# Linear attention and squared-ReLU MLP in one kernel: the written-out order of all five engines replaced by another

## Chip, cores and metric

One core of a Trainium2 chip runs the whole program. The metric is the device time of one execution in microseconds (us), as a median over executions. Engine names are those of the profile: PE is TensorE, PEld its weight loads, DVE is VectorE, ACT is ScalarE, POOL is GpSimd, SP is SyncE, which here issues the DMAs.

## What is computed

```python
def phi(x):                                  # x: 8 batches, 8 heads, 576 tokens, 64 wide
    proj = einsum('bhsd,df->bhsf', x, w_phi) # 128 features
    proj = proj - max(abs(proj), axis=-1, keepdims=True)
    return concatenate([exp(proj), exp(-proj)], axis=-1)
q_p, k_p = phi(q), phi(k)
kv = einsum('bhsf,bhsd->bhfd', k_p, v)
z = sum(k_p, axis=2)
num = einsum('bhsf,bhfd->bhsd', q_p, kv)
den = einsum('bhsf,bhf->bhs', q_p, z)[..., None] + 1e-06
x = (num / den) as 4608 tokens x 512
g = maximum(x @ w_in, 0) ** 2                # w_in 512 x 2048
out = g @ w_out                              # w_out 2048 x 512
```

## The kernel before

The work is cut into items. `P.add` records an item with its engine, a duration that the planner assumes, the items it must follow, the buffers and PSUM banks it uses, and a class of TensorE use (WHOLE, ROWS, COLS, STRIPS: the whole array, or parts of its rows or columns). There are 3676 items, 590 of them on PE. Nothing is scheduled at run time: the string ORDER holds two characters for each item, its place in one list over all engines, and the string WAYS holds one digit for each item that can run on more than one engine. `Plan.order` sorts the items by place; each engine then executes its own in that sequence, and the Tile layer puts semaphore waits where the data or a buffer demand one. So an engine that waits holds up everything behind it on that engine. DMAs all go out from SP, in the same fixed sequence.

Attention goes by 32 pairs of heads. Pairs 0 to 5 (`early`, lines 607 to 742) are done while the weights are still being prepared. For each: `k_main` and `k_tail` (L532, L538) and `q_main` and `q_tail` (L655, L661) multiply keys and queries by w_phi; DVE takes the row maxima and subtracts them (L548, L551, L559, L562 for keys, L666, L668 for queries); ACT makes the exponentials of the keys (L554, L556, L565, L567); `kv_main` and `ends` (L594, L599, L627) make kv and z; `flip` (L639) and `q_turn` (L689, L693) transpose; ACT makes the exponentials of the queries out of PSUM (L698, L700); `num` and `dens` (L708, L725) make numerators and denominators. The next product into the PSUM pair `pp` must wait until L698 and L700 have read it. Pairs 6 to 31 (`visit`, `late`) do the same with larger items between the MLP's.

Also in the first 100 us the 16 blocks of the MLP's weights (1 MB each, tiles raw0i to raw7i and raw0o to raw7o) are loaded and brought into split form: ACT and POOL each process the raw words (L399, L402), DVE joins them (L406), POOL and DVE write the parts (L442, L249, L460, L471, L474). `power` (L341 on PE, then four small DVE instructions L347, L348, L351, L352) finds a power of two to scale two weight blocks by.

The MLP runs over 18 chunks of 256 tokens. The first four go by `gemm1` (L956, 24 matmuls) and `gemm2` (L993, 12 matmuls); the other 14 go in pairs by a block scheme with seven products instead of eight (`step`, L1161) and `gemm2`. Intermediate halves are put away to memory and read back by SP.

In `tile_kernel`'s last lines, where the plan leaves a gap of over 0.7 us on PE in the first 125 us and a PSUM bank is free, matmuls on a zero tile (`zeros`, L1332) are put into it; the first eight such matmuls (`warm`, L359) stand at the very start.

```python
        order = sorted(self.ops, key=lambda op: place[op.n])
...
            if last and last.end < FILL_TO and op.start - last.end > 0.7:
                gaps.append((last.end, op.start))
...
        fills.append((t0, lambda tag=free[0], n=n, count=int(0.6 * (t1 - t0) / 0.214): zeros(tag, n, count)))
```

Of the kernel before, what the change touches and what calls it, by code (L numbers as in the profile page):

```python
# [235 lines left out]
def tile_kernel(ctx, tc, qp, kp, vp, w_phi, w_in, w_out, out):  # L236
    nc = tc.nc
    V, A, G, PE, SP = nc.vector, nc.scalar, nc.gpsimd, nc.tensor, nc.sync
    P = Plan()
# [365 lines left out]
    def early(p):  # L605
# [26 lines left out]
        o = P.add("PE", 1.7, lambda: kv_main(p, pv_["s", p]), exps[p] + [v_load[p]], kv[:-1], R(2.0), mode=COLS)  # L632
        o = P.add("PE", 1.76, ends, [o, exp_t[p]], kv, R(2.5), mode=(COLS, STRIPS))
# [48 lines left out]
        for c in range(2):  # L682
# [13 lines left out]
            o = P.add("PE", 0.7, q_turn, [pool_start] + less[:2 + c], [pq, ("pt", p)], R(x), mode=(WHOLE, ROWS if c else WHOLE))  # L696
# [104 lines left out]
    def visit(i):  # L801
# [60 lines left out]
        if n is not None:  # L862
            v3 = visited[0] = P.add("PE", 2.04, numerators, [kz_of[n]] + qexp[n], use_n, R(0.0), mode=COLS)
# [80 lines left out]
    def moe(c, f, turn, n, m, po):  # L944
# [15 lines left out]
        g1 = P.add("PE", 2.61, gemm1, after, [("ph", bank), (f"w{f}", 0)], m)  # L960
# [20 lines left out]
    def second(n, c, v, f, turn, g, rank, po):  # L981
# [189 lines left out]
    def step(cs, k, turn, f, n, m):  # L1171
# [193 lines left out]
    "#k#s#z#}$&#?#F#n#V#x$9$D$M$$$:$<$]$e$i%(%.%6%>%2%;%=%R%V%j%}&*&8!b#Q#(#W#8#=#E#|#N#`#r$+#^#m$4$5$2$;"
    "$L$c$o$,$?$f$b$j$u%#%%$m$y%)%-%8%B%h&$%m&&%M%T%X%d%g%r&-&3&6#q#a$B$F$6$C$v&4&h&}($(B*}#J$K#f$*#{$)$I"
    "$Q$#$1$@$k$.$0$N$z$w$}%0%C%N$p%&%4%7%:%<%H%K%b%l%n%q%x&!&9&>&5&n&(&,&/&:&Y&l(%(|)#(x)0#c%D$E$Z$O$R%5"
    "%E$U$X$r%1$[$^$n$t%Q%Z%e&+&0&1&?&A&F&L&B&U&Z&O&S&W&^&e&g(-(3(K(R(G(L(Z(i(m(z)D)L)Q)S)x$J%I%G%@%P%U%_"
    "%i%Y%^%s%v%L%a%c%p%u&)&%%F(4(8&k%y(>(F(H&y&|(0&z(((.(;()(,(9(D&X&p&_&s)&);),&M(`(?(o(v(})$)()))5)F)]"
# [107 lines left out]
```

## Time and profile before

| what | us |
|---|---|
| median of 3 executions | 1010.53 |
| lowest and highest | 1009.52, 1014.01 |
| the profiled execution | 1009.59 |
| its span, first to last instruction | 1007.8 |
| PE busy (with modelled ends) | 993.1 |
| DVE, ACT, POOL busy | 801.9, 605.3, 352.5 |

Busy times are unions of an engine's instructions. Matmuls are pipelined and their ends are modelled, so a matmul that was held up for less than its own pipeline's length shows no idle time; starts are exact, and from the start of one item to the start of the next is the time that the item took on PE.

### The profile page before, as it was taken

The numbers are of one execution on the slowest core, as the hardware profiler recorded it, in microseconds if no ns is written. First come the engines' busy times: TensorE is split into PE (matmuls) and PEld (weight loads), VectorE is DVE, ScalarE is ACT, GpSimd is POOL, SyncE is SP. The second block draws the span as 40 slices with busy tenths as digits, with TensorE's granted clock in tenths as the row PEclk, the third lists the DMA queues.
The fourth block names the chain that finished last, engine by engine and source line by source line (L and its number), as shares of the span: only waits on it lengthen the run. The fifth ranks groups of instructions, "written<-read, shape, count | busy, mean of one in ns | idle before, by whom it ended". The sixth has DMA issues, their size and how long they took to land.

```text
span 1007.8 us, 19886 instructions
## 1 busy us (share of the span) xinstructions
PE 993.1 (99%) x7552; PEld 676.4 (67%) x7552; DVE 801.9 (80%) x1417; ACT 605.3 (60%) x1140; POOL 352.5 (35%) x141
## 2 busy tenths in 40 slices
PE   9899999999999999999999999999999999999998
PEld 5666666666677776676657775677567756766774
DVE  6899888899997788887898988778878775773543
ACT  6798876766654576477765775476825552441232
POOL 2562366556510154443373543533452420000000
PEclk9999999999999999999999999999999999999999
DMA  9865532542235776667676685568756655666321
GB/s 340 300 193 181 170 95 81 156 146 71 60 114 164 215 230 197 211 196 218 211 200 202 192 272 173 175 184 245 207 149 185 193 180 191 223 203 216 105 84 42
DMA packets 149543, 180.60 MB, mean 179 GB/s; under 512 B 76872, under 2 KB 97352, under 8 KB 147400
## 3 DMA queue, kind: packets, MB, share of 16 engines
q1 hardware_dynamic: 149160, 178.81, 57.6%
q8 instruction: 59, 0.97, 0.4%
q10 hardware_dynamic: 288, 0.52, 0.1%
q14 instruction: 36, 0.29, 0.1%
HBM read 137.93 MB, written 41.21 MB: 178 GB/s over the span
## 4 chain that ended last, share of the span: by engine, by line
PE 82%; DVE 7%; issue 4%; DMA 2%; ACT 2%; POOL 1%; SPq 0%; POOLq 0%; DVEq 0%; ACTq 0%
PE po L993 32%; PE ph L1161 9%; PE ph L956 7%; PE pv L1161 6%; PE pn L1161 6%; PE pz L594 4%; PE pn L830 2%; PE pp L532 2%; PE pp L1161 2%; PE pn L809 2%; PE pv L830 2%; POOL rb L927 1%; PE pz L599 1%; PE pv L993 1%; PE pn L993 1%
## 5 line engine op out<-in xcount | busy, mean ns | idle before, releaser
L1161 PEld LDWEIGHTS <-w 128*128 128x128 f16 x2352 | 224.5, 98 | 49.5 <-issue 23.0
L906 POOL PARTITION_ALL_REDUCE mx<-pt x52 | 114.5, 2201 | 267.1 <-ACT pt L253 118.1
L993 PE MATMUL po<-wh,gh 128*128 128x512 f32 x544 | 174.1, 441 | 0.0
L1212 ACT ACTIVATE w<-w,cw 128x512 f32<-128x512 f32 x112 | 77.7, 713 | 116.7 <-DVE w L1167 113.2
L993 PE MATMUL po<-wl,gh 128*128 128x512 bf16 x544 | 140.8, 380 | 1.0 <-DMA gh<-gd 0.6
L993 PE MATMUL po<-wl,gl 128*128 128x512 bf16 x544 | 139.8, 379 | 0.2 <-DVE gl L249 0.2
L927 POOL PARTITION_ALL_REDUCE rb<-rb x26 | 97.6, 3756 | 110.3 <-DVE rb L924 99.0
L993 PEld LDWEIGHTS po<-wh,gh 128*128 128x128 f32 x544 | 102.7, 189 | 31.3
L973 ACT ACTIVATE gh<-w 128x512 fp32r<-128x512 f32 x112 | 69.2, 624 | 72.8 <-PE po L993 38.1
L927 POOL PARTITION_ALL_REDUCE ds<-ds x26 | 96.3, 3703 | 29.5 <-DVE ds L924 29.3
L993 PEld LDWEIGHTS <-gl 128*128 128x128 bf16 x576 | 56.3, 98 | 68.4 <-DVE gl L249 0.9
L249 DVE TENSOR_TENSOR gl<-w,gh 128x512 bf16<-128x512 f32 x112 | 82.5, 744 | 19.8 <-ACT w L975 18.9
L993 PEld LDWEIGHTS <-gh 128*128 128x128 bf16 x576 | 51.2, 98 | 59.2 <-issue 18.6
L956 PE MATMUL ph<-ring,w 128*128 128x256 f16 x768 | 89.4, 273 | 0.6 <-ACT r L965 0.4
L1161 PE MATMUL ph<-ring,w 128*128 128x256 f16 x624 | 85.6, 273 | 0.0
L956 PEld LDWEIGHTS <-w 128*128 128x128 f16 x768 | 72.9, 98 | 17.9 <-issue 9.9
L1161 PE MATMUL pv<-w,w 128*128 128x256 f16 x576 | 70.8, 273 | 0.3 <-ACT pt L253 0.3
L580 DVE TRANSPOSE_TENSOR_REDUCE z<-e 128x32 f32<-128x1024 f32 x52 | 63.9, 1232 | 0.0
L1167 DVE TENSOR_TENSOR w<-pv,w 128x512 f32<-128x512 f32 x96 | 53.0, 552 | 8.5 <-PE pv L1161 6.4
L911 ACT ACTIVATE qe<-qe 128x576 f32<-128x576 f32 x52 | 35.3, 679 | 31.4 <-DVE qe L249 29.7
L1167 DVE TENSOR_TENSOR w<-pn,w 128x512 f32<-128x512 f32 x48 | 32.8, 682 | 25.2 <-PE pn L1161 22.6
L976 DVE TENSOR_TENSOR w<-w 128x512 f32<-128x512 f32 x33 | 23.4, 711 | 36.6 <-ACT gh L973 36.5
(256 smaller groups left out, 1859.4 us busy)
## 6 DMA issues: line engine op xcount, KB each, us to landing
w<-wd SPq DMA_DIRECT2D x112, 512.0 KB, 4.6
gd<-gh SPq DMA_DIRECT2D x48, 256.0 KB, 3.6
gh<-gd SPq DMA_DIRECT2D x48, 256.0 KB, 3.4
v<-in_vp_dram SPq DMA_DIRECT2D x32, 320.0 KB, 4.2
q<-in_qp_dram SPq DMA_DIRECT2D x32, 288.0 KB, 3.6
k<-in_kp_dram SPq DMA_DIRECT2D x32, 288.0 KB, 4.4
rb<-rd SPq DMA_DIRECT2D x64, 144.0 KB, 3.6
out_dram<-o SPq DMA_DIRECT2D x34, 256.0 KB, 4.4
```

The lines of the kernel that those rows point to most:

```text
L249: eng.tensor_tensor(out=out_, in0=a, in1=b_, op=ALU.subtract)
L580: sums[p].append(P.add("DVE", dve_us(256 * k), lambda: V.tensor_reduce(out=col(), in_=src().rearrange("p k (b x) -> p k b x", x=32), op=AL ...
L594: PE.matmul(out=to[64 * h:64 * h + 64, 0:256], lhsT=v_at(p)[:, t, h, :], rhs=e_[2 * p + h][:, t].rearrange("p s f -> p (s f)"), start=t == ...
L830: PE.matmul(out=to[64 * h:64 * h + 64, :], lhsT=kz_[n][:, 128 * s_ + 64 * h:128 * s_ + 64 * h + 64], rhs=qe_[2 * n + h].rearrange("p (s x) ...
L906: o = P.add("POOL", par_us(S), lambda n=n, h=h: G.partition_all_reduce(mx_[n - EARLY], pt_[p][:, h, :], channels=128, reduce_op=bass_isa.R ...
L927: o = P.add("POOL", 3.6, lambda y=y: G.partition_all_reduce(y(), y(), channels=128, reduce_op=bass_isa.ReduceOp.add), [o], [home], R(RQ + ...
L956: PE.matmul(out=ph[:, j, :], lhsT=w_[f][0][:, w, t, 128 * j:128 * j + 128], rhs=at_ring(c, x, t), start=k == 0, stop=k == 3 * KT - 1)
L973: sq = P.add("ACT", act_us(512), lambda: A.activation(out=gh_[n], in_=r(), func=AF.Square), after, use + [("gh", n)], Q)
L993: PE.matmul(out=bank(i), lhsT=x[:, j, 128 * i:128 * i + 128], rhs=w[:, j, :], start=turn + j + s == 0, stop=(turn, j, s) == (NFP - 1, 1, 2))
L1161: PE.matmul(out=to, lhsT=fl(x, *al)(k), rhs=fr(y, *ar)(k), start=n == 0, stop=n == 5)
L1167: V.tensor_tensor(out=to, in0=a, in1=b, op=ALU.add)
L1212: x = P.add("ACT", act_us(512, 1), lambda i=i: A.activation(out=r()[:, 2 * i:2 * i + 2, :], in_=r()[:, 2 * i:2 * i + 2, :], func=AF.Relu, ...
```

## The change

The durations that some PE items are planned with are changed, and ORDER and WAYS are replaced whole. The item times enter only the placement of the zero matmuls; no computation differs. Of the 590 PE items most keep their neighbours: some 60 to 70 are moved, most of them by one to three places.

```diff
-        km = P.add("PE", 0.95, lambda: k_main(p, k_to), [k_load[p], ld_w], [("k", p)] + k_use, R(0.0), mode=ROWS)
+        km = P.add("PE", 1.02, lambda: k_main(p, k_to), [k_load[p], ld_w], [("k", p)] + k_use, R(0.0), mode=ROWS)
...
-        o = P.add("PE", 1.7, lambda: kv_main(p, pv_["s", p]), exps[p] + [v_load[p]], kv[:-1], R(2.0), mode=COLS)
-        o = P.add("PE", 1.76, ends, [o, exp_t[p]], kv, R(2.5), mode=(COLS, STRIPS))
+        o = P.add("PE", 1.78, lambda: kv_main(p, pv_["s", p]), exps[p] + [v_load[p]], kv[:-1], R(2.0), mode=COLS)
+        o = P.add("PE", 1.7, ends, [o, exp_t[p]], kv, R(2.5), mode=(COLS, STRIPS))
...
-        g1 = P.add("PE", 2.61, gemm1, after, [("ph", bank), (f"w{f}", 0)], m)
+        g1 = P.add("PE", 2.632, gemm1, after, [("ph", bank), (f"w{f}", 0)], m)
...
-        g2 = P.add("PE", 2.64, gemm2, [g] + list(w_done[f, False]), [("gh", n), ("gl", n)] + po, rank)
+        g2 = P.add("PE", 2.663, gemm2, [g] + list(w_done[f, False]), [("gh", n), ("gl", n)] + po, rank)
...
 ORDER = (
-    "!$!#!!!(!)!+!9!4!=!M!`!e!g!j$7&q!,!P!N!V![!-!X!W!^!w#>#B#]#d#I#p!a#!###)#-#4#M!?#&!p#,#1!{#o#S#u#y$!"
+    "!&!#!!!(!)!+!/!7!<!L!U!X!Y!`$8)J!,!O!P!S!W!1!e!c!o!v#<#B#H#f#[#q!_#$#%#*#.#5#N!:#)!t#-#3!s#n#D#t#z$$"
```

SP, the first loads of the program (`wraw` is w_phi, `q`, `k`, `v` are pairs 0 to 3, `raw` the weight blocks). Before:

```order
L325 DMA wraw<-in_w_phi_dram 128x768
L525 DMA q_168<-in_qp_dram 128x576
L524 DMA k_170<-in_kp_dram 128x576
L487 DMA v_172<-in_vp_dram 128x640
L487 DMA v_174<-in_vp_dram 128x640
L524 DMA k_176<-in_kp_dram 128x576
L487 DMA v_178<-in_vp_dram 128x640
L383 DMA raw0i<-in_w_in_dram 128x2048
L383 DMA raw1i<-in_w_in_dram 128x2048
L524 DMA k_225<-in_kp_dram 128x576
```

Of the change:

```order
L525 DMA q_167<-in_qp_dram 128x576
L524 DMA k_169<-in_kp_dram 128x576
L325 DMA wraw<-in_w_phi_dram 128x768
L487 DMA v_172<-in_vp_dram 128x640
L487 DMA v_174<-in_vp_dram 128x640
L524 DMA k_176<-in_kp_dram 128x576
L487 DMA v_178<-in_vp_dram 128x640
L383 DMA raw0i<-in_w_in_dram 128x2048
L525 DMA q_192<-in_qp_dram 128x576
L487 DMA v_194<-in_vp_dram 128x640
L383 DMA raw1i<-in_w_in_dram 128x2048
L524 DMA k_229<-in_kp_dram 128x576
```

w_phi is loaded behind q and k of pair 0, and q of pair 1 and v of pair 3 go ahead of the second weight block. On PE the four zero matmuls between `warm` and the first L655 are gone; in all there are 8 zero matmuls where there were 14.

POOL, the preparation of the first weight blocks (`wh`, `wl` are the parts of one block). Before:

```order
L442 CAST wh_471<-u_421 128x1024
L249 TENSOR_TENSOR wl_489<-u_421,wh_471 128x1024
L402 TENSOR_SCALAR raw3i<-raw3i 128x1024
L460 CAST wl_489<-u_421 128x1024
L402 TENSOR_SCALAR raw1o<-raw1o 128x1024
```

Of the change:

```order
L442 CAST wh_470<-u_427 128x1024
L249 TENSOR_TENSOR wl_487<-u_427,wh_470 128x1024
L402 TENSOR_SCALAR raw1o<-raw1o 128x1024
L460 CAST wl_487<-u_427 128x1024
L402 TENSOR_SCALAR raw3i<-raw3i 128x1024
```

raw1o and raw3i have changed places; on SP their loads have too: before raw3i, raw4i, raw1o, now raw4i, raw1o, raw3i.

PE, from the end of pair 1's query transposes (L689, L693 into `pp`) to `ends` of pair 2 (`pv`; the L532 into `po` are pair 4's keys). Before, with the rows that repeat left out:

```order
L693 MATMUL pp_576<-ident,pt_476 128x64 x2
L1332 MATMUL pv_589<-o_135 128x512
...
L532 MATMUL po_606<-wraw,k_552 128x128
L532 MATMUL po_608<-wraw,k_552 128x128
...
L594 MATMUL pv_622<-e_403,v_178 64x256
L594 MATMUL pv_622<-e_431,v_178 64x256
...
L599 MATMUL pv_622<-et_556,v_178 64x256 x2
```

Of the change:

```order
L693 MATMUL pp_573<-ident,pt_483 128x64 x2
L594 MATMUL pv_587<-e_414,v_178 64x256
L594 MATMUL pv_587<-e_430,v_178 64x256
...
L532 MATMUL po_610<-wraw,k_549 128x128
L532 MATMUL po_612<-wraw,k_549 128x128
...
L599 MATMUL pv_587<-et_553,v_178 64x256 x2
```

Three zero matmuls are gone, and pair 2's kv product stands ahead of pair 4's keys.

## Rows read from the trace of the kernel before

**Rows 1.** Busy time by stretch: stretch us, its length, engines, clock, DMA share, GB/s.
```profile
0.00:60.00 60.00, 53.82 (x602) 35.88 (x602) 48.28 (x95) 45.95 (x88) 26.22 (x24) 0.97 0.86 304
60.00:125.00 65.00, 63.91 (x630) 42.59 (x629) 60.65 (x103) 55.59 (x98) 22.84 (x14) 1.00 0.54 175
300.00:500.00 200.00, 199.66 (x1505) 138.44 (x1504) 164.48 (x309) 127.38 (x248) 66.03 (x23) 1.00 0.66 201
sum 1008.00, PE 993.11 PEld 676.40 DVE 801.95 ACT 605.34 POOL 352.46; mean PE 141.87 PEld 96.63 DVE 114.56 ACT 86.48 POOL 50.35
```
**Rows 2.** Who waited for whom, PE: us in total, times, longest.
```profile
PE pn L661 <- DVE et L562: 1.7, 1, 1.7
```
**Rows 3.** Timeline of PE, the start: start us, duration us, instructions.
```profile
4.56 1.81 PE L1332 MATMUL pp<-o 128*128 128x512 bf16 x4
6.30 0.37 PE L655 MATMUL ph<-wraw,q 64*128 64x128 f32 x1
```
**Rows 4.** The load of pair 0's keys on SP: issue time, and us to landing.
```profile
L524 SPq DMA_DIRECT2D k<-in_kp_dram x1: 423/423/423, 1.6 to 1.6; - x1
...
DMA to landing us min/median/max: 4.0/4.0/4.0
```
**Rows 5.** Timeline of DVE: its first product work, and small instructions of two scalings.
```profile
7.49 0.69 DVE L666 TENSOR_REDUCE qm<-ph 128x4 f32<-128x512 f32 x1 [5.98 <-PE ph L655]
...
20.19 0.15 DVE L348 TENSOR_SCALAR pw<-pw 128x1 int32<-128x1 int32 x1
...
30.79 1.13 DVE L348 TENSOR_SCALAR pw<-pw 128x2 int32<-128x2 int32 x1
31.96 1.04 DVE L351 TENSOR_SCALAR cw<-pw 128x2 f32<-128x2 f32 x1
```
**Rows 6.** Timeline of POOL, the same stretch (in brackets: idle before, and its releaser).
```profile
30.74 1.16 POOL L402 TENSOR_SCALAR raw3i<-raw3i 128x1024 int32<-128x1024 uint32 x1
...
33.17 1.11 POOL L402 TENSOR_SCALAR raw1o<-raw1o 128x1024 int32<-128x1024 uint32 x1 [0.19 <-DMA raw1o<-in_w_out_dram]
```
**Rows 7.** Timeline of PE: pair 3's keys, the zero matmuls, pair 4's keys.
```profile
24.68 1.11 PE L532 MATMUL po<-wraw,k 64*128 64x128 f32 x16
...
36.86 1.46 PE L1332 MATMUL pv<-o 128*128 128x512 bf16 x3
38.26 2.08 PE L532 MATMUL po<-wraw,k 64*128 64x128 f32 x16
```
**Rows 8.** Busy time by stretch around the half clock (columns as rows 1).
```profile
31.50:36.80 5.30, 2.76 (x26) 1.52 (x24) 5.10 (x14) 3.56 (x6) 3.68 (x4) 1.00 0.80 285
36.90:40.20 3.30, 3.30 (x21) 2.03 (x19) 3.30 (x5) 3.27 (x7) 1.09 (x1) 0.50 0.54 128
```
**Rows 9.** Timeline of ACT: the read of pair 4's v.
```profile
49.56 0.74 ACT L493 ACTIVATE sx<-v 128x640 bf16<-128x640 f32 x1 [1.60 <-DMA v<-in_vp_dram]
```
**Rows 10.** Timeline of SP: that load's issue, and the store of pair 1's denominators.
```profile
42.01 1.50 SPq L487 DMA_DIRECT2D v<-in_vp_dram  x1
45.35 0.58 SPq L734 DMA_DIRECT2D den<-mx  x1
```
**Rows 11.** Timeline of PE: pair 5's keys, and pair 1's first numerators.
```profile
51.52 1.16 PE L532 MATMUL pp<-wraw,k 64*128 64x128 f32 x16 [0.32 <-ACT qe L700]
53.53 1.19 PE L708 MATMUL pn<-qe,kz 128*64 128x288 f32 x8 [0.85 <-DVE pt L668]
```
**Rows 12.** Timeline of PE: two second products (L993), each with the item behind it.
```profile
105.30 1.03 PE L993 MATMUL po<-wl,gh 128*128 128x512 bf16 x4
...
108.05 1.19 PE L708 MATMUL pn<-qe,kz 128*64 128x288 f32 x8
...
140.73 1.03 PE L993 MATMUL po<-wl,gh 128*128 128x512 bf16 x4
...
143.39 2.79 PE L956 MATMUL ph<-ring,w 128*128 128x256 f16 x24
```
**Rows 13.** Who waited for whom, SP, from 150 us on: us in total, times, longest.
```profile
SPq L1091 <- PE ph L1161: 62.7, 18, 9.9
```

More of the change, by code (lines that the diff above doesn't have):

```diff
@@ L695, in early @@
             x = 1.3 + 1.5 * c
-            o = P.add("PE", 0.7, q_turn, [pool_start] + less[:2 + c], [pq, ("pt", p)], R(x), mode=(WHOLE, ROWS if c else WHOLE))
+            o = P.add("PE", 0.73, q_turn, [pool_start] + less[:2 + c], [pq, ("pt", p)], R(x), mode=(WHOLE, ROWS if c else WHOLE))
             src = lambda n=n, c=c: pp_["q", n][:, :, 32 * c:32 * c + SH]
@@ L862, in visit @@
         if n is not None:
-            v3 = visited[0] = P.add("PE", 2.04, numerators, [kz_of[n]] + qexp[n], use_n, R(0.0), mode=COLS)
+            v3 = visited[0] = P.add("PE", 1.99, numerators, [kz_of[n]] + qexp[n], use_n, R(0.0), mode=COLS)
             for bank, key, lo, hi in ((pn_, pn, 0, N0), (pv_, pv, N0, S)):
@@ L1193, in step @@
         two = lambda i, x, y: lambda: (product(banks[i]()[:, 0, :], *x), product(banks[i]()[:, 1, :], *y))
-        pa = P.add("PE", 0.66, lambda: product(banks[0]()[:, 0, :], "a11", "b11"), after, keys[0] + reads, m)
+        pa = P.add("PE", 0.667, lambda: product(banks[0]()[:, 0, :], "a11", "b11"), after, keys[0] + reads, m)
         first, other = copy(T, lambda: r()[:, 1, :], lambda: banks[0]()[:, 0, :])
@@ L1365 @@
[L1365 to L1369, printed above, removed]
@@ new lines @@
+    "&>%O&@&E%Z&I%u&U&]&m((&J&b&a&g&k&p&w(&(.(L(]&Y&y&q(;(B&o(6(1(A(I(O(`(R(W(d(Y!%!$!4!0!8!;!>!B!=!@!E!H"
+    "!2!5!A!G!M!T!Z!b!f!-!3!6!C!F!h!j!l!J!R!m!}#,#/!r!z#I#R#1#8#=#]#a#k$9$w%d!*!.!D!?!K!N!^!i!Q!]!a!q!I!V"
+    "!|#!!x#(#:#?#C![!g#2!u#4#Q#S#U#7#E#O#Y#s#u$S$W$N$Y#w$!$&$?$B$f%#%M%h!9!k!d#G!y!{#0#V###&#;#@#K#L#Z#m"
+    "#_#o#v#{$/#A#P#l#W#y$5$A$O$#$3$C$a$j$v%(%/%8%@%2%:%=%N%Q%i%{&3&7!n#c#+#X#6#>#d#x#F#b#h#j#`#p#|$%$6$<"
+    "$F$^$h$,$D$i$e$m${%$%%$x%)%*%.%<%D%n%}%k&#%J%R%U%c%e%p&&&0&5$+#M$E$L$>$c$n%b&.(!(%(a)W#J$G#i$*#}$($:"
@@ new lines @@
+    "$K$-$4$=$M$0$2$Q$t$l$|%1%G%P$q%&%6%9%>%?%B%F%f%l%o%s%w%|&8&<&4&t&$&*&-&L&P&`&{(r)3(l)%#r%A$H$Z$P$V$]"
+    "$r$T$[$p%7$`$d%3%4%T%_%g&)&+&/&=&D&H&K&B&G&T&O&W&Z&_&f&i(-(5(J(S(F(Q(T(m(o(u).)r){)g)u$1%E%L%C%V%X%`"
+    "%t%]%a%j%q%H%Y%[%^%y&(&%$_&[(8&l%x(=(C(K&z&}(0&r()(/(4&|(+(9(D&u(2&x(G(n)>)<&h(<(@(b(p(v)!)$)))7)D)]"
+    "({)*)2)6)B)K)i)t*(*,*2%v(V([(3(N)-)?)9)G)a)c(s(})C(E(H(^)/(j(t(w(y(i)4(k)8)k*5)y*O*]*b*X*e)A)X)R)j);"
+    ")U)b)h)l*$*)*=)[)o*#*%***/*@*P*Z*^*k&2&e(Z(|(c)F)N)Y)`)d)f+B3|(>*H)m*3)=)s)z)v*8*R*a)H)L*-*A*C*G*I*E"
@@ L1442 @@
+    "0000000000000000100001110100010000010100000010000001100100100100100001011100001010010000100000001101"
+    "0000000010001000100000001000110011101101000000000010000001001000000001010110000001001101100010111001"
+    "0010001010110011001101100010000100001011101010101"
 )
```

154 lines of the change are left out of this document (73 added, 81 removed).

## Prediction

> **What bounds the kernel now.** I read the busy time by stretch first [rows 1]. PE is busy 993.11 of 1008.00 us, so a new order has at most about 15 us of visible idle time to win, and what it can win lies early: 6.18 us of the first 60 are idle (60.00 less 53.82) and 1.09 of the next 65, while from 300 to 500 us only 0.34 are. The reader is to see two more things there. The clock is below 1 in the first stretch alone. And DVE, with 48.28 and 60.65 us, is nearly as full as PE in the first two stretches, so PE waits there for DVE and an earlier PE item helps only if DVE is earlier too. The waits of PE say the same: the longest is that of L661, the query tail of pair 1, 1.7 us behind DVE [rows 2]. Then come the timelines of PE, DVE, POOL, ACT and SP up to 60 us, place by place, since each place has its own limit.
>
> **The change part by part.** The matmuls are the same. So I go through the places where the order or a load moved and ask who is late there afterwards. All starts are of the profiled execution, 1009.59 us, of which 1007.8 is the span; the median shown, 1010.53, is 0.94 above it.
>
> *Start.* Four zero matmuls of 1.81 us stand ahead of the first query product, which starts at 6.30 [rows 3]. They are gone. The product now needs q, k and w_phi of the first three loads; before, the third load, issued at 1.6, landed 4.0 later, at 5.6 [rows 4]. The three move the same bytes in another sequence, so I keep 5.6: PE starts 0.7 earlier. DVE's first instruction is now the maximum of the key tail, which needs one more small product: before, DVE began 1.19 behind the first query product (7.49 less 6.30) [rows 3, 5]; with some 0.3 to 0.4 more, DVE begins at 7.1 to 7.2, 0.35 earlier. From there DVE does the same work in nearly the same sequence, so **0.35 us** is what goes on, with 0 and 0.7 as ends. What is gone with the zero matmuls is their cover: PE idles from about 4.8 to 5.6. Whether its clock comes up as early as before no row can show; between it and no effect at all I take no effect, since DVE, not PE, sets the pace up to 40 us.
>
> By the Trainium skill, "TensorE: Matmul & The Clock Gate" (What's actually happening), the slow clock is the default state and activity ends it, so the removed zero matmuls could delay full speed. By that rule the first three products, about 2.5 us together at full speed, would take up to 2.5 more, and the 0.35 won would turn into a loss.
>
> *Scaling of the first weight blocks, 30 us.* Two small DVE instructions took 1.13 and 1.04 us there, where one of their kind took 0.15 at 20.19 [rows 5]. The first ended when POOL's raw3i instruction did (30.74 and 1.16) [rows 5, 6]. The excess is 1.13 + 1.04 less 2 x 0.15, or **1.87 us**, and PE's 1.7 us of waiting hangs on it [rows 2]. After the change the DVE instructions between the join of raw0o and this place are the same in number and kind, and so are POOL's two before; POOL's next is raw1o in place of raw3i. If raw1o has landed when POOL is free, it runs at the same moment and the delay stays. Before, raw1o landed at 33.17, third of the three blocks [rows 6]; it is now second of three, and the queue ahead of it is about 1 us early. One block took about 2.5 to 3 us of transfer, as an estimate from three blocks between about 25 and 33.17, so it lands at 29 to 31, and POOL is free at about 30.3. This is near an even chance; I put 0 in the sum and keep 1.87 as the other end.
>
> The Trainium skill, "SBUF — State Buffer" (Who interferes with whom), states that DVE and POOL share a port pair as an exclusive lock, that whoever starts first holds it for the whole instruction, and that a tensor_scalar takes part and a reduction doesn't. By that rule the delay goes to nothing if raw1o lands even slightly late; the sum would then be 1.87 lower. The trace agrees as to the size.
>
> *Pair 2's kv ahead of pair 4's keys, 37 us.* Before, three zero matmuls ran from 36.86 and pair 4's keys from 38.26, in 2.08 us where the same item took 1.11 at 24.68 [rows 7]. The granted clock was 0.50 from 36.90 to 40.20, the lower level of 1.2 GHz, after a stretch in which PE was busy 2.76 of 5.30 us [rows 8]. So 3.4 us went by (36.86 to about 40.3) for an item worth 1.1. The change runs the kv product there, whose exponentials ACT has done by then, and the keys behind it, without zero matmuls: at full clock that saves 2.3 us. If the idle stretch before stays (the delay above), the clock will probably fall again, and 3.3 us at half speed now fall on real work and cost 1.65; then the saving is 0.7. I take **1.5**, between the two.
>
> *Pair 4's v, 42 to 52 us.* Pair 5's keys wait until ACT has read `pp` (0.32 us of waiting at 51.52) [rows 11], and ACT had been held by the load of pair 4's v until 49.56 [rows 9]. That load went out at 42.01 [rows 10], 7.5 us before. It now stands behind the store of pair 1's denominators, which went out at 45.35 [rows 10]; with PE some 2 to 3 us earlier there, the store goes at about 42.4 and v at about 43. One 1 MB block ahead of it starts earlier too, so v lands 5.5 to 7 us on, at 48.5 to 50, and the keys start 2 us behind that, at 50.5 to 52, as before they did (51.52 less 49.56). Against 51.52 that caps all that was won so far at 1.0, and can turn it to -0.5. I take **0.8** for everything up to here: this is where the gain of the two places above goes.
>
> *Numerators of pair 1.* The 0.85 us wait at 53.53 for DVE [rows 11] is on the bank that holds pair 2's query tail; that tail now runs an item earlier and the other bank's numerators go first. One item of 1.19 covers the wait: **0.85** won, 0 as the other end if DVE is no earlier.
>
> *The rest.* Where a whole-array item is followed by one of another class, the second product took 2.75 us to the next start (108.05 less 105.30), and 2.66 with its own class behind it (143.39 less 140.73) [rows 12]. I counted the changes of class along PE's order: 167 before, 176 now. Nine at 0.09 cost **0.8**. Against that stand several waits and hold-ups of 0.2 to 0.8 us beyond 60 us; some of the moves lie at them, most don't. I take **1.3** won, with 0 and 3 as ends. SP, POOL, ACT and DVE moves not named lie beside PE work and are put at nothing; the cover is that PE's next items are ready, and where it is gone it costs the wait itself, as below.
>
> Sum: -0.8 - 0.85 + 0.8 - 1.3 is about -2.2 us from 1009.59, so 1007.4 for an execution like the profiled one. Medians lie up to 0.9 above it: **1007.7**.
>
> **Rivals.** A measurement of this kernel can tell about 0.5% (5 us) from no change.
>
> 1. *Both early knots open.* The 1.87 us are gone, so PE has no idle stretch, the clock stays up (2.3), v lands at 48 and caps nothing, and both later terms hold: 0.35 + 1.87 + 2.3 + 0.85 less the part that overlaps (PE's 1.7 of waiting is the same time as DVE's, and DVE must follow), about 4.4, and 3 - 0.8 later: -6.6, 1003. For it: the loads moved the right way. Against it: DVE's 48.28 of 60 leaves little to move into.
> 2. *DVE paces it anyway.* Up to 125 us DVE has the same sum of work, 109 us; PE's moves only trade waits. Then the gain is the start's 0.35, the class changes cost 0.8: 1010. The change would then not do what it is for. For it: DVE was idle only for short spells up to 44 us.
> 3. *A late load in the block stage (slower).* SP issues in order, and in front of the weight loads of the steps (L1091) it sat 62.7 us in 18 waits, the longest 9.9 [rows 13]. Where a moved item puts such a load behind one more wait of 3.5 us (62.7 / 18) than its slack allows, PE's step stands still for the difference. Two such places cost 7 us: 1017. It decides from the point where the slack of a load is under 3.5 us. Against it: from 300 to 500 us PE lacks only 0.34, and the moves there are small.
> 4. *The start's clock or v's load, slower by little.* Up to 2.5 at the start, or v landing at 52: 1011 to 1012.5.
>
> **How the numbers follow.** The forecast has 0.36, rival 1 0.27, rival 2 0.20, rival 3 0.08, rival 4 0.09. Faster by over 0.5% (under 1005.5) is rival 1 and a little of the forecast's lower side, 0.29; slower (over 1015.6) is rival 3, 0.08; the rest, 0.63, is within 0.5%. The range goes from 1002.5, which leaves out the lower end of rival 1, to 1012.5, which leaves out rival 3: together under 2 in 10.
>
> **What would show it.** Right: the first query product at about 5.6; one wait of PE before pair 5's keys near 50 us; the kv product directly behind L693; class changes still at 0.09. The delay of DVE's L348 and L351 near 30 us tells the forecast from rival 1, as does a clock of 0.50 near 37 us. Wrong: PE idle time over 1 us at any place after 150 us, or pair 5's keys before 49 us.

## The result

The changed kernel is slower: 1018.83 us as a median of 9 executions (1014.06 to 1021.75), against 1010.53 (1009.01 to 1014.48) of the kernel before on the same chip. The ratio is 1.0071, with a 95% interval of 1.0047 to 1.0094. The profiled execution took 1019.26 us, its span 1017.5, where before it was 1009.59 and 1007.8. The prediction of 1007.7 had the sign wrong, and its range ended at 1012.5.

Busy time by stretch, the kernel before; this stretch is not among [rows 1], whose columns it has:

```profile
125.00:300.00 175.00, 173.59 (x1316) 119.26 (x1315) 159.43 (x294) 116.45 (x224) 92.44 (x31) 1.00 0.37 104
```

The same view of the changed kernel:

```profile
0.00:60.00 60.00, 53.78 (x592) 35.89 (x596) 46.49 (x96) 45.56 (x88) 26.25 (x24) 1.00 0.87 307
125.00:300.00 175.00, 168.81 (x1262) 116.35 (x1275) 153.03 (x274) 116.12 (x227) 91.36 (x31) 0.99 0.39 108
300.00:500.00 200.00, 197.16 (x1464) 138.44 (x1484) 169.12 (x316) 121.42 (x237) 66.16 (x23) 1.00 0.64 194
```

The reader is to see that the first 60 us, of which nearly all of the prediction spoke, came out alike (53.78 against 53.82 in [rows 1]), and that PE is idle 6.19 us of 125 to 300 where it was idle 1.41. Of the 6.19, 5.0 are waits; the other 1.2 stand at L993, 87 of whose 1728 matmuls have no record in this trace. The waits of PE from 120 us on, in the kernel before (us in total, times, longest):

```profile
PE pp L532 <- DVE ds L924: 1.4, 2, 0.7
PE po L993 <- DMA gh<-gd: 0.6, 1, 0.6
```

and in the changed kernel:

```profile
PE ph L956 <- ACT r L965: 2.2, 3, 1.1
PE pp L532 <- DVE ds L924: 2.0, 1, 2.0
...
PE ph L1161 <- DVE w L254: 1.6, 1, 1.6
PE po L993 <- DMA gh<-gd: 1.6, 2, 1.1
PE ph L1161 <- DVE w L1167: 0.9, 1, 0.9
```

Comparing the start of each PE item in the two traces gives where the time went. The changed kernel is 3.9 us behind at 15 us and still at 30, 0.1 at 42, 0.9 from 80 to 125, then 4.8 at 178, 5.7 at 280, 8.6 at 450, 7.5 at 750 and 9.6 at the last product. These are two single executions. So there are three things to explain: a start that lost 4 us, a gain of 4 us between 30 and 42, and 9 us lost after 125, the largest piece within 10 us at 173.

**The start.** Timeline of PE, the changed kernel [rows 3]:

```profile
7.45 0.55 PE L655 MATMUL ph<-wraw,q 64*128 64x128 f32 x1 [2.68 <-DMA wraw<-in_w_phi_dram]
10.08 2.08 PE L532 MATMUL po<-wraw,k 64*128 64x128 f32 x16
```

The third load, now w_phi, ended PE's wait at 7.45, and L532 takes 2.08 us where [rows 7] has 1.11 for the item. The clock has no record there before 13.5 us, so the duration itself is the reading: in the run early_zeros below the same L532 took 2.08 us while the granted clock was recorded as 0.50, the level of 1.2 GHz. PE had been idle for 2.68 us.

**30 to 42 us.** DVE [rows 5], POOL [rows 6], PE [rows 7] and the stretches [rows 8] of the changed kernel:

```profile
34.55 0.17 DVE L348 TENSOR_SCALAR pw<-pw 128x2 int32<-128x2 int32 x1
34.76 0.17 DVE L351 TENSOR_SCALAR cw<-pw 128x2 f32<-128x2 f32 x1
```
```profile
34.76 1.22 POOL L402 TENSOR_SCALAR raw1o<-raw1o 128x1024 int32<-128x1024 uint32 x1
```
```profile
38.66 0.28 PE L693 MATMUL pp<-ident,pt 64*128 64x64 f32 x2
38.87 1.95 PE L594 MATMUL pv<-e,v 128*64 128x256 f32 x16
```
```profile
31.50:36.80 5.30, 5.30 (x61) 3.63 (x53) 5.16 (x13) 5.26 (x11) 5.08 (x4) 1.00 1.01 402
36.90:40.20 3.30, 2.50 (x23) 1.70 (x24) 2.44 (x8) 2.52 (x5) 3.06 (x4) 1.00 0.65 230
```

The two small DVE instructions take 0.17 us each instead of 1.13 and 1.04, PE is busy all 5.30 us instead of 2.76, and the clock stays at full speed. In part this is the luck of the two executions. The runs mid_new, swap_two and swap_behind below have the order of before up to 106 us, and in their traces L348 is held too (0.90 to 1.09 us), but the clock has no stretch at 0.50 near 37 us; in late_new's it has.

**173 us.** DVE, POOL and PE of the changed kernel, and the stretch behind:

```profile
168.66 0.81 DVE L924 SCALAR_TENSOR_TENSOR rb<-qe,zc,pp 128x576 f32<-128x576 f32 x1
169.40 3.08 DVE L1075 TENSOR_TENSOR ring<-w 128x256 f32<-128x256 f16 x2
172.40 0.80 DVE L924 SCALAR_TENSOR_TENSOR ds<-qe,zc,pp 128x576 f32<-128x576 f32 x1
```
```profile
169.57 3.69 POOL L927 PARTITION_ALL_REDUCE rb<-rb  x1 [7.64 <-DMA q<-in_qp_dram]
```
```profile
173.26 1.47 PE L532 MATMUL pp<-wraw,k 64*128 64x128 f32 x16 [2.04 <-DVE ds L924]
175.56 2.80 PE L594 MATMUL pz<-e,v 128*64 128x256 f32 x16
```
```profile
173.97:177.38 3.41, 3.41 (x31) 2.42 (x30) 3.27 (x7) 1.03 (x2) 0.00 (x0) 0.50 0.02 7
```

In the kernel before, the pair L1075 stood behind the second L924:

```profile
170.23 0.81 DVE L924 SCALAR_TENSOR_TENSOR ds<-qe,zc,pp 128x576 f32<-128x576 f32 x1 [0.49 <-ACT pp L922]
171.32 0.71 DVE L1075 TENSOR_TENSOR ring<-w 128x256 f32<-128x256 f16 x2
```
```profile
168.68 3.59 POOL L927 PARTITION_ALL_REDUCE rb<-rb  x1 [7.83 <-DVE rb L924]
```
```profile
171.10 1.16 PE L532 MATMUL pp<-wraw,k 64*128 64x128 f32 x16 [0.68 <-DVE ds L924]
```

The first L924 releases POOL's reduction L927, which begins at 169.57. The second instruction of the pair L1075, with both inputs in SBUF, begins at 169.73, 0.16 us inside it, and ends at 172.48, 0.8 us before the reduction's recorded end. The second L924 is behind it on DVE, and PE's keys L532 wait for that. PE idles 2.04 us, and from 173.97 on the clock is at 0.50 for 3.41 us: L594 takes 2.80 instead of the 1.90 to 1.95 that it has elsewhere.

The same pattern stands at three later places: at 284 us L1075 took 3.09 us under POOL's L927, at 430 us L249 (qe) 2.54, and at 806 us L249 (gl) 3.11, each with an instruction behind it that PE, or ACT for PE, waited for. The last one, DVE, POOL and PE:

```profile
805.88 3.11 DVE L249 TENSOR_TENSOR gl<-w,gh 128x512 bf16<-128x512 f32 x1 [1.65 <-ACT w L975]
808.92 0.41 DVE L254 COPY w<-ph 128x256 f32<-128x256 f32 x1
```
```profile
805.84 3.67 POOL L927 PARTITION_ALL_REDUCE ds<-ds  x1
```
```profile
809.38 0.82 PE L1161 MATMUL ph<-w,w 128*128 128x256 f16 x6 [1.63 <-DVE w L254]
```

The kernel before has such held instructions as well. Counting the DVE instructions past 125 us that took at least 0.5 us longer than the median of their line and shape, it has 31, all beside a reduction of POOL, with 32.9 us of excess in all; the changed kernel has 28, with 34.2 us. So the holds are not more. What differs is what stands behind them.

The planner in the kernel knows this hold: `Plan.order` lengthens whichever of the two comes second (`locked`). Evaluated with the item times of the change, it lets the pair L1075, to the planner one item of 0.84 us, begin at 169.63 and L927 at 169.67. So it plans the pair unheld and makes L927 4.40 us long. On the chip the pair is two instructions, and the second came behind L927's start. At 430 and 806 us too the plan has DVE ahead, by 0.09 and 0.45 us, where in the trace it is behind, by 0.67 and 0.04.

The theory to test: these places make the late loss; the start costs by itself; the gain at 30 to 42 us is real and pays for the start. In the expectations a **hold-up** is the time from one PE item's start to the next less the usual time of such a pair of items, and an **item** is one entry of ORDER.

### The profile page after: what moved, and what is told of

It is laid out like the page before. It is cut to its first block, busy times and chain, and to the rows that moved or that the text cites. A ratio compares the mean times of both kernels' runs of the same rounds, so it can differ in the third digit from the quotient of the medians.

```text
span 1017.5 us, 19773 instructions
## 1 busy us (share of the span) xinstructions
PE 988.8 (97%) x7457; PEld 678.4 (67%) x7546; DVE 798.7 (78%) x1422; ACT 601.8 (59%) x1133; POOL 354.9 (35%) x143
## 4 chain that ended last, share of the span: by engine, by line
PE 80%; DVE 7%; DMA 5%; issue 3%; ACT 2%; POOL 1%; POOLq 0%; SPq 0%; DVEq 0%; ACTq 0%
PE po L993 31%; PE ph L1161 9%; PE ph L956 7%; PE pn L1161 5%; PE pv L1161 5%; PE pz L594 4%; PE pn L830 3%; PE pp L532 3%; PE pn L809 2%; PE pp L1161 2%; PE pv L830 2%; DMA den<-ds 1%; PE pz L599 1%; PE pn L993 1%; PE pv L993 1%
## 5 line engine op out<-in xcount | busy, mean ns | idle before, releaser
L906 POOL PARTITION_ALL_REDUCE mx<-pt x52 | 116.6, 2242 | 251.3 <-DVE pt L254 84.9
L993 PE MATMUL po<-wh,gh 128*128 128x512 f32 x544 | 174.2, 441 | 0.0
L993 PE MATMUL po<-wl,gl 128*128 128x512 bf16 x543 | 139.8, 379 | 0.3
L927 POOL PARTITION_ALL_REDUCE rb<-rb x26 | 95.6, 3676 | 121.5 <-DVE rb L924 105.0
L993 PE MATMUL po<-wl,gh 128*128 128x512 bf16 x462 | 125.7, 380 | 7.3 <-issue 1.9
L993 PEld LDWEIGHTS po<-wh,gh 128*128 128x128 f32 x544 | 102.7, 189 | 31.3
L249 DVE TENSOR_TENSOR gl<-w,gh 128x512 bf16<-128x512 f32 x112 | 83.1, 746 | 48.7 <-ACT w L975 47.8
L927 POOL PARTITION_ALL_REDUCE ds<-ds x26 | 96.1, 3697 | 39.8 <-DVE ds L924 24.8
L993 PEld LDWEIGHTS <-gl 128*128 128x128 bf16 x576 | 56.3, 98 | 68.4 <-DVE gl L249 0.6
L993 PEld LDWEIGHTS <-gh 128*128 128x128 bf16 x576 | 51.2, 98 | 60.3 <-issue 16.3
L554 ACT ACTIVATE e<-e 128x512 f32<-128x512 f32 x64 | 39.7, 624 | 30.0 <-DVE e L551 29.7
L975 ACT ACTIVATE w<-w 128x512 f32<-128x512 f32 x86 | 53.3, 623 | 1.3
L1167 DVE TENSOR_TENSOR w<-pn,w 128x512 f32<-128x512 f32 x48 | 32.9, 686 | 22.7 <-PE pn L1161 18.7
```

The lines of the kernel that those rows point to most:

```text
L249: eng.tensor_tensor(out=out_, in0=a, in1=b_, op=ALU.subtract)
L906: o = P.add("POOL", par_us(S), lambda n=n, h=h: G.partition_all_reduce(mx_[n - EARLY], pt_[p][:, h, :], channels=128, reduce_op=bass_isa.R ...
L927: o = P.add("POOL", 3.6, lambda y=y: G.partition_all_reduce(y(), y(), channels=128, reduce_op=bass_isa.ReduceOp.add), [o], [home], R(RQ + ...
L975: o = P.add("ACT", act_us(512), lambda: A.activation(out=r(), in_=r(), func=AF.Square), [sq], use, Q, other=[("DVE", 0.70, lambda: V.tenso ...
L993: PE.matmul(out=bank(i), lhsT=x[:, j, 128 * i:128 * i + 128], rhs=w[:, j, :], start=turn + j + s == 0, stop=(turn, j, s) == (NFP - 1, 1, 2))
L1167: V.tensor_tensor(out=to, in0=a, in1=b, op=ALU.add)
```

## Experiments

### Which stretch, and order or division

The two orders can be joined at a place: the first so many items of one, then what is left in the other's sequence. Item 455 stands at about 106 us, item 1178 at about 300.

```
early_new:  items up to 455 as changed, rest as before
late_new:   items up to 455 as before,  rest as changed
mid_new:    up to 455 as before, up to 1178 as changed, rest as before
order_new:  ORDER as changed, WAYS as before (194 of 549 divisions undone)
```

> The first 455 items (to about 106 us) in the changed order with its divisions, the rest in the order and divisions of before. Theory (the loss is made after 106 us, by DVE work held up at places where the new order leaves TensorE no slack): TensorE reaches the cut about 0.9 us later than before (106.18 against 105.30 in the two traces), and nothing is lost behind it, so about 1010 to 1012 us, within 0.2% of before. Rival 1 (the late start is what costs, and shifts everything behind it into collisions): about 1017 to 1019 us, as the whole change. Rival 2 (the loss is spread over the program by more changes of TensorE class): half way, about 1012 to 1014.

> The first 455 items as before, the rest in the changed order with its divisions. Theory: nearly the whole loss is here, about 7 to 8 us: 1016 to 1019 us, and TensorE loses some 6 us between 125 and 300 us, with the wait near 173 us and the ones from 263 to 290 us. Rival 1 (the start): about 1010 us.

> Before up to 106 us, the changed order and divisions from there to about 300 us (items 455 to 1178), then before again. Theory: the stretch from 106 to 300 us makes about 6 of the 8 us: 1015 to 1017 us. Rival 1 (the start): 1010. Rival 3 (the losses after 300 us, at 433, 809 and 912 us, weigh as much): 1012 to 1013.

> The changed order of all engines throughout, but each of the 194 items whose engine the change swaps (ACT, DVE or POOL) stays on the engine that it had before. If the order of the items makes the loss (theory): 1016 to 1020 us. If the swapped divisions make it (rival 4): 1009 to 1012 us. An order and a division that were searched together may also fit badly when they are parted; then it is slower than both, over 1021 us, and says little.

Measured, as ratios to before: early_new 1.0019 (1.0010 to 1.0029), late_new 1.0067 (1.0053 to 1.0081), mid_new 1.0042 (1.0029 to 1.0054), order_new 1.0084 (1.0069 to 1.0099). So most of the loss is behind 106 us, 4 of 7 us of it before 300, where 6 were expected. It is there with the start of before as well, which ends the rival that the late start propagates. The hold-up at 173 us stands in the traces of late_new, mid_new and order_new alike, 2.17 to 2.42 us. Nothing points to the swapped divisions: with those of before it is no faster, though an order parted from its divisions may lose by that alone. But early_new costs 2 us too, although at 106 us its trace is only 0.1 us behind before, and at 400 us level with it. Its profiled execution lost 2.1 us behind 400, where its order is that of before, 1.5 of them to two loads that landed later than before:

```profile
404.31 1.04 PE L993 MATMUL po<-wl,gh 128*128 128x512 bf16 x4 [0.71 <-DMA gh<-gd]
```
```profile
829.55 1.04 PE L993 MATMUL po<-wl,gh 128*128 128x512 bf16 x4 [1.23 <-DMA gh<-gd]
```

So the 2 us of early_new are measured, but its trace doesn't lead them back to the first 106 us.

### DVE under POOL's reduction

undo_fill and undo_locks move items of the changed kernel; swap_two and swap_behind move one of before.

```diff
 undo_fill, DVE of the changed kernel
 L924 SCALAR_TENSOR_TENSOR rb
-L1075 TENSOR_TENSOR ring x2
 L924 SCALAR_TENSOR_TENSOR ds
 L967, L580, L548, L551
+L1075 TENSOR_TENSOR ring x2
 swap_two, DVE of before
-L249 TENSOR_TENSOR ring
 L924 SCALAR_TENSOR_TENSOR rb
+L249 TENSOR_TENSOR ring
 swap_behind, DVE of before
-L249 TENSOR_TENSOR ring
 L924 SCALAR_TENSOR_TENSOR rb
 L580 TENSOR_REDUCE z
+L249 TENSOR_TENSOR ring
 L924 SCALAR_TENSOR_TENSOR ds
```

> The changed kernel with one DVE item moved: the addition that the planner calls fill (L1075, tile ring, at 169.40 us in the changed kernel's trace) goes from right behind the first L924 (rb) to five items later, behind L548 and L551 of the next keys. Theory (DVE's L1075 sits out POOL's L927, 3.08 us instead of 0.7, with the second L924 behind it, and TensorE's L532 waits for that): TensorE's hold-up near 173 us falls from 2.21 to about 0.8, the clock does not fall there, and the kernel is 2.5 to 4 us faster than the changed one, 1015 to 1016.5 us. Rival (what is late there is L924's other input, or the time is lost at the next place anyway): no difference, 1018 to 1020 us.

> The kernel before with two neighbours on DVE exchanged: a subtraction L249 (ring, 0.68 us at 167.18) that ran just ahead of the first L924 (rb) runs just behind it, where POOL's L927 begins. Theory: L249 now lasts until POOL's L927 ends, some 3 us, the second L924 (ds) is that much later, TensorE's L532 near 171 us is held up 2 to 2.5 us instead of 0.84, the clock falls for a while, and the whole is 2.5 to 4 us slower than before: 1012.5 to 1014 us. Rival (the hold-up needs the rest of the new order): 1010 us, no change.

> As swap_two, but the subtraction L249 (ring, 0.68 us) runs one instruction later still on DVE, behind L580 and just ahead of the second L924 (ds). In swap_two it started 0.17 us before POOL's L927, was not held, and POOL's L927 took 3.96 us instead of 3.59. Theory: now it starts well inside POOL's L927, so it ends only when that ends (about 172 us on the trace of before), the second L924 comes some 2 us later, TensorE's L532 near 171 us is held up by 2.3 to 3 us instead of 0.84, the clock falls for 3.4 us as in the changed kernel, and the whole is 2 to 4 us slower than before: 1012 to 1014 us. Rival (position does not matter, only the sum of DVE's work does): 1010 us.

> The changed kernel with two more places mended as in undo_fill, by moving items on DVE and ACT alone: near 284 us the pair L1075, L249 (ring) goes behind L249 (gl), and ACT's L1079 behind L965 (r); near 430 us L249 (qe) goes behind L1167. Theory: besides the hold-up at 173 us those of 1.3 at 289.8 and 0.9 at 433 us go, so 1.5 to 2.2 us less than undo_fill (1014.8): 1012.6 to 1013.5 us. Rival (each lost place is made up for at the next one): as undo_fill, 1014 to 1015 us.

Measured: undo_fill 1.0057 (1.0030 to 1.0084), median 1014.80; undo_locks 1.0032 (1.0016 to 1.0048), median 1013.45; swap_two 0.9993 (0.9981 to 1.0004); swap_behind 1.0008 (0.9995 to 1.0020). In undo_fill PE's keys L532 no longer wait:

```profile
173.72 0.59 PE L809 MATMUL pv<-q,wraw 64*128 64x512 f32 x1
174.35 1.16 PE L532 MATMUL pp<-wraw,k 64*128 64x128 f32 x16
```

The place is cured, and the median is 4.0 us lower, as expected; by the ratio it is 1.4, with intervals that overlap, since this kernel's executions lie between 1012 and 1023. The three places together, undo_locks, give 3.9 us by the ratio, with intervals that just touch; by the medians it is 5.4, as expected, but only the ratios compare with the kernel before on the same chip. In undo_locks's trace PE's waits near 284 and 430 us are gone, although the instructions that were moved are still held there (L1075 3.09 us, L249 1.94): PE waits for nothing behind them any more.

swap_two is a miss that told more than a hit. DVE and POOL:

```profile
166.70 0.68 DVE L249 TENSOR_TENSOR ring<-ring 128x512 f16<-128x512 f32 x1
```
```profile
166.87 3.96 POOL L927 PARTITION_ALL_REDUCE rb<-rb  x1 [7.22 <-DVE rb L924]
```

Directly behind L924 the subtraction begins 0.17 us before POOL does. It is not held, and it is POOL's reduction that takes 3.96 us instead of the 3.59 that it took at this place before. One instruction later, in swap_behind, it is DVE that waits:

```profile
168.39 2.09 DVE L249 TENSOR_TENSOR ring<-ring 128x512 f16<-128x512 f32 x1
170.40 0.80 DVE L924 SCALAR_TENSOR_TENSOR ds<-qe,zc,pp 128x576 f32<-128x576 f32 x1
```
```profile
167.40 3.59 POOL L927 PARTITION_ALL_REDUCE rb<-rb  x1 [7.23 <-DVE rb L924]
```
```profile
171.26 1.16 PE L532 MATMUL pp<-wraw,k 64*128 64x128 f32 x16 [1.49 <-DVE ds L924]
```

So who begins first holds the other, and in the changed kernel it is the second instruction of the pair L1075 that comes too late. In swap_behind PE waited 1.49 us instead of 0.68, the clock did not fall there, and the kernel is 1.5 us slower than swap_two by the ratios. That is the 0.8 of the wait and some that the two intervals cannot resolve; against before swap_behind's own interval reaches to no change. The 2 to 4 expected counted a fall of the clock. It came behind PE's idle 2.04 us in the changed kernel and not behind 1.49 here, but the length of the idle time alone does not decide: in after_wfirst below PE idled longer at this place, and the clock stayed up.

```profile
174.47 1.16 PE L532 MATMUL pp<-wraw,k 64*128 64x128 f32 x16 [2.27 <-DVE ds L924]
```

The Trainium skill, "SBUF — State Buffer" (Who interferes with whom), states just this: a DVE instruction with two SBUF inputs contends with a GpSimd one that reads SBUF, and the one that issues first has the shared ports for its whole length. The traces agree on both orders of starting; the held instruction ended 0.5 us before the reduction's recorded end in swap_behind, and 0.8 before it in the changed kernel. They agree as well that one input in PSUM is enough to escape: in the kernel before, the second L924, with `pp` in PSUM, began at 170.23, 1.55 us inside L927, and took its 0.81 us.

### The place at 30 us alone

```diff
 pool_swap, POOL of before
-L402 TENSOR_SCALAR raw3i
+L402 TENSOR_SCALAR raw1o
 L460 CAST wl
-L402 TENSOR_SCALAR raw1o
+L402 TENSOR_SCALAR raw3i
```

> The kernel before with one exchange on POOL: the L402 of raw1o goes ahead of the L402 of raw3i (the zero matmuls stay where they were). In the trace of before raw1o landed at 33.1 us, and POOL is free at 30.7; so POOL waits for it, and DVE's L348 and L351 at 30.8 us find no POOL instruction running. Theory (DVE's small instructions there were held by POOL's L402 of raw3i): L348 and L351 take 0.17 us instead of 1.13 and 1.04, TensorE's hold-up of 1.86 at 34.5 us goes, the clock does not fall near 37 us, and TensorE is some 2 us ahead at 45 us, of which 1 to 2 reach the end: 1008.5 to 1009.5 us. Rival (DVE's work before L348 is what is late, POOL is not the cause): as before, 1010 us. Against both: raw3i is 3 us later, which could hold up the weights after 60 us and give the gain back.

Measured: 0.9988 (0.9972 to 1.0003), median 1009.57. DVE and POOL:

```profile
31.18 0.17 DVE L348 TENSOR_SCALAR pw<-pw 128x2 int32<-128x2 int32 x1
31.38 0.17 DVE L351 TENSOR_SCALAR cw<-pw 128x2 f32<-128x2 f32 x1
```
```profile
34.10 1.14 POOL L402 TENSOR_SCALAR raw1o<-raw1o 128x1024 int32<-128x1024 uint32 x1 [3.34 <-DMA raw1o<-in_w_out_dram]
```

What held the two instructions is shown: POOL waits 3.34 us for raw1o, and L348 and L351 run at their own length. The clock has no stretch at 0.50 near 37 us, but neither has it in three traces in which L348 was held, so the clock is not shown to hang on this. The time is 1.2 us lower by the ratio, which the interval does not quite tell from nothing.

### The start

knot_only joins as above: before up to item 102 (26 us), changed up to 455, then before. The others are early_new with an edit:

```diff
 early_zeros
+fills.insert(0, (2.0, lambda: zeros("pp", 99, 4)))
 early_wfirst, SP (the planner's rule then puts four zero matmuls ahead of the first L655)
+L325 DMA wraw<-in_w_phi_dram
 L525 DMA q<-in_qp_dram
 L524 DMA k<-in_kp_dram
-L325 DMA wraw<-in_w_phi_dram
 early_wnozero, as early_wfirst, and
+fills.pop(0)
```

> As early_new (the first 455 items in the changed order, the rest as before), with four zero matmuls put back ahead of the first query product. In early_new's trace that product started at 5.72 us but ran at the lower clock until 10.2 us. If the missing zero matmuls hold the clock down (theory): full clock from the first product or soon after, L532 at about 8 us in 1.16 us instead of 2.03, TensorE 1 to 2 us earlier at 15 us; at the end at most 1 us of it is left, since DVE sets the pace up to 30 us: 1010 to 1011.4 us. If the clock does not hang on them: the first product 0.6 us later, 1011.5 to 1012 us.

> Before up to its 102nd item (about 26 us), the changed order from there to item 455 (about 106 us), then before again: the changed order's treatment of the places at 30 to 42 us without its start. In the changed kernel's trace these places give TensorE back 4 us (it was 3.9 us behind before at 30 us and 0.1 at 42). If that gain stands on its own (theory): TensorE is 1.5 to 3 us ahead of before at 45 us, and since the load of pair 4's v and the places from 60 to 75 us take some of it, 1008 to 1009.5 us, 0.5 to 2 us faster than before. Rival (the 4 us were only the late start caught up with, DVE being the limit in both): 1010 us, as before.

> As early_new (the first 455 items changed, the rest as before), but w_phi is the first load again, ahead of q and k of pair 0; the planner's rule then puts zero matmuls ahead of the first product again too. early_new took 1011.4 us, early_zeros (zero matmuls back, w_phi third) 1011.3, knot_only (the start of before, the changed order from 26 us) 1008.6. Theory (the late landing of w_phi, 5.7 to 7.7 us in the traces with it third, and the lower clock of the first products cost some 2 to 3 us, more in some executions than in others): 1008.5 to 1009.5 us, with as little spread as knot_only. Rival (what costs is the loads of q and v of pairs 1 and 3 ahead of the second weight block): as early_new, 1011 to 1011.5 us.

> As early_wfirst, without the four zero matmuls ahead of the first query product. It tells the load's place from the zero matmuls. If the place of w_phi's load decides (theory): the first product at 5.0 to 5.7 us, ratio as early_wfirst, 0.998 to 0.999. If the zero matmuls decide by the clock: the first products at the lower clock as in early_new (L532 in 2.03 us, full clock from about 10 us), ratio 1.000 to 1.002.

Measured: early_zeros 1.0003 (0.9987 to 1.0020), knot_only 0.9990 (0.9982 to 0.9999), early_wfirst 0.9979 (0.9963 to 0.9995), early_wnozero 1.0005 (0.9991 to 1.0020), beside 1.0019 of early_new. PE in early_new, and in early_wfirst:

```profile
5.72 0.55 PE L655 MATMUL ph<-wraw,q 64*128 64x128 f32 x1 [0.95 <-DMA wraw<-in_w_phi_dram]
8.35 2.03 PE L532 MATMUL po<-wraw,k 64*128 64x128 f32 x16
```
```profile
5.75 0.37 PE L655 MATMUL ph<-wraw,q 64*128 64x128 f32 x1
7.21 1.16 PE L532 MATMUL po<-wraw,k 64*128 64x128 f32 x16
```

With the same first start the lower clock alone puts L532 1.1 us later. knot_only, the changed order from 26 to 106 us with the old start, is as its theory had it, but by the ratio 1.0 us faster than before, not the 4 that the trace showed between 30 and 42 us. Both halves of the start undone give 4.0 us by the ratios (2.1 by the medians) and the best kernel of all, 0.9979, two us faster than before. Either half alone gives 1.4 to 1.6 us, which its interval does not tell from nothing. In early_zeros w_phi landed late, PE idled 1.68 us behind the zero matmuls, and the clock fell all the same:

```profile
9.00:12.30 3.30, 3.08 (x22) 2.20 (x22) 2.44 (x6) 1.16 (x4) 0.28 (x1) 0.50 1.02 422
```

In early_wnozero the first products ran slowly from 4.70 us on, 0.42 us each instead of 0.27, and L532 at full speed from 7.65. So neither half alone kept all of the first products at full speed. How the two share the cost stays open, and so does how it reaches the end: early_new and early_wfirst are both within 0.1 us of before at 106 us and at 400, while early_zeros, with the lower clock behind 9 us, was 2.8 behind at 106 and 2.6 at the end.

### All of it mended

```diff
 after_wfirst: the changed kernel, and
+L325 as the first DMA on SP
 all_mended: after_wfirst, and
+the DVE and ACT moves of undo_locks
```

> The changed kernel with all mended that the runs so far blame: w_phi as the first load again (with the zero matmuls that the planner's rule then puts ahead of the first product) and the three places of undo_locks on DVE and ACT. By the ratios to before, early_new 1.0019 against early_wfirst 0.9979 makes the start worth 0.0040, and undo_locks stands at 1.0032. Theory (the start and the held DVE instructions are the whole loss, and they add up): about 0.999, 1009 to 1011 us beside a before of 1010.5. Rival (the rest of the new order costs too, or the two overlap): 1.002 or more, 1012.5 to 1014 us.

> The changed kernel with w_phi as the first load again (and the zero matmuls that the planner's rule then puts ahead of the first product), nothing else undone. Theory (start and late places add up): 3 to 4 us faster than the changed kernel, ratio 1.0031 to 1.004, 1013.5 to 1015 us, with the hold-up at 173 us still there. Rival (the late places set the end alone, an early gain is waited away at 173 us): as the changed kernel, 1.006 to 1.007.

Measured: after_wfirst 1.0055 (1.0037 to 1.0074), all_mended 1.0025 (1.0011 to 1.0039). all_mended is as its rival had it: the two causes do not add up to the whole. after_wfirst lies between its theory and its rival, and its interval reaches into both. Against each other the two are the clearest test of the held instructions, since they ran on one chip: 3.0 us by the ratios, and ten of all_mended's twelve executions are below the lowest of after_wfirst's six. w_phi first, on the other hand, is worth 1.6 us by the ratios in the changed kernel and 0.7 in undo_locks, which the intervals do not tell from nothing. after_wfirst's trace was 2.1 us ahead of before at 45 us and 1.9 behind at 112, which is earlier than all the mended places. The waits of PE from 60 to 115 us there, the two longest:

```profile
PE pv L594 <- DVE kz L254: 1.1, 1, 1.1
PE pp L532 <- ACT qe L700: 1.0, 1, 1.0
```

The first of them, for DVE's copy into kz, stands in eight of the eleven traces of kernels with the changed order from 26 to 106 us, 0.62 to 2.70 us long, and in none with the order of before. It is the same hold again. The changed order has DVE's small L743 ahead of that copy, and in those eight L743 took 1.07 to 2.31 us beside an instruction of POOL instead of 0.17; in the order of before it stands behind the copy. The longest, in undo_fill, DVE, POOL and PE:

```profile
71.39 2.31 DVE L743 TENSOR_SCALAR den<-den 128x9 f32<-128x9 f32 x1
```
```profile
70.48 3.20 POOL L249 TENSOR_TENSOR wl<-u,wh 128x1024 bf16<-128x1024 f32 x1
```
```profile
74.42 3.02 PE L594 MATMUL pv<-e,v 128*64 128x256 f32 x16 [2.70 <-DVE kz L254]
```

The clock was at 0.50 from 75.14 to 78.55, and undo_fill, level with before at 70 us, was 4.0 behind at 106, in an execution of 1019.33 us. In the changed kernel's own trace L743 began 0.01 us ahead of POOL's L402 (72.02 against 72.03) and took 0.17; in early_new it began 0.07 behind it (70.32 against 70.25) and took 1.10. So this fifth place comes and goes from trace to trace, and no run mended it.

In all_mended the place at 806 us is left (PE idle 1.6 us): its copy writes a tile `w` behind the held subtraction, which reads one, and it was not moved. Its profiled execution took 1009.35 us, the fastest of its twelve, with L743 at 0.17, so no trace shows what the one of 1016.01 lost. That 2.5 us remain is measured; which places make them is not.

## Why the prediction was wrong

**The rest** is the step that failed. It took a gain of 1.3 us with 0 to 3 as ends, and the program lost some 7 us there (late_new). The working put the moves on DVE, ACT, POOL and SP "at nothing", with the cover "that PE's next items are ready". At 173 us that cover was 0.68 us of waiting already, so there was none: one pair of DVE instructions moved ahead of L924 cost 2.0 us of wait and 0.9 on the next L594. The same lock had been costed at 30 us, with 1.87 us from two rows, but was not looked for at the other places where the order sets a two-input DVE instruction beside a POOL reduction. Moving DVE and ACT items at three of these places took back 3.0 us (after_wfirst against all_mended) to 3.9 (the changed kernel against undo_locks); what makes the others stays open in part. No loss was allowed as an end, so the range stopped short.

**Start.** The term was 0.35 won, with the clock at no effect. The landing of the third load is no fixed 5.6: over six traces with this head of the queue PE's wait for it ended between 5.69 and 7.76, at 7.45 in the changed kernel's. DVE's first product work came at 10.20 instead of 7.1, and the clock was low. Rival 4 had this. The rule of the Trainium skill, "TensorE: Matmul & The Clock Gate" (What's actually happening), that activity ends the slow clock, had the sign: without the zero matmuls L532 took 2.03 us in early_new, with them 1.16 in early_wfirst. The 0.35 won became a loss; by the ratios it is 4.0 us where it is undone in early_new, and 0.7 to 1.6, not told from nothing, where it is undone in the whole change.

**Scaling at 30 us.** The end of 1.87 came true, not the 0 in the sum. In pool_swap the reason is the one that was weighed, raw1o landing late. In the changed kernel it is another: POOL itself was 4 us late, and L348 began at 34.55, 0.21 ahead of POOL's L402 at 34.76. In all eleven traces with the changed order from 26 to 106 us L348 took 0.17.

**Pair 2's kv.** Right: L594 begins 0.21 us behind L693, without zero matmuls, and the clock holds, so against the execution of before that was read the 2.3 us end applies rather than 1.5. In mid_new, swap_two and swap_behind, with the order of before here, the clock did not fall either, so part of the 2.3 was never the order's to win. With the place at 30 us this is rival 1; in these two traces its 4 us went into the late start, and knot_only, without that start, kept 1.0.

**Pair 4's v.** As predicted in effect: the store went out at 45.94, the load at 46.58, and pair 5's keys began at 51.98, within 50.5 to 52; but no wait of PE stands before them.

**Numerators of pair 1.** The wait of 0.85 at L708 is gone, but one of 0.51 stands behind it at L538 (55.75), so about 0.3 was won.

**Class changes.** Summing the median time of each kind of item, by its own class and the next one's, over both orders gives, as an estimate, 0.44 us more, where 0.8 was taken. No run tried it alone.

**Rival 3** had the sign and the size, 1017, by another mechanism: no wait of PE on a weight load's transfer is among its longest after 120 us. Its point, a slack used up by something moved ahead in a fixed queue, was the right one on the wrong queue. Of the two signs named beforehand, PE idle over 1 us after 150 us came, at 173, 290, 809 and 912 us; at 912 it was a load gh<-gd, as in early_new.

## What to carry to other kernels

When a fixed order is replaced, list the places where the engine that bounds the kernel already waits, however little, and read on the feeding engine what now stands ahead of the item waited for. An instruction that is short alone can take as long as a neighbour engine's reduction if it begins inside it, so what counts is what it begins beside and what waits behind it, not its length: both kernels have about thirty held instructions past 125 us, and a few places make the difference. Where a plan lets one engine be first by hundredths of a microsecond, count on the other outcome as well. And cost a start by what it does to the clock as well as by the landing of its last load, with the landing as a range, and ask how much of it is still there 100 us later.

## Not expected of the hardware

The subtraction that began 0.17 us ahead of POOL's reduction made the reduction 0.37 us longer (3.96 against 3.59) and lost nothing itself; one that began inside it was stretched from 0.68 to 2.09 us. And at one place, about 173 us, PE's clock fell to 0.50 for 3.41 us behind 2.00 to 2.25 us of idle time in four kernels (the changed one, late_new, mid_new, order_new), and stayed up behind 1.49 in swap_behind and 2.27 in after_wfirst.
